# Attention weights of batches 1 to 7 transposed by DMA instead of TensorE, in a fused sliding-window attention and feed-forward kernel

## The chip, the cores and the metric

The kernel runs on one core of a Trainium2 chip. The metric is device time in microseconds; before the change it was 381.18 us (median of 3 runs, 380.14 to 381.52). The engines are called PE (TensorE, matmul), DVE (VectorE), ACT (ScalarE), POOL (GpSimd) and SP (SyncE, which here only issues DMAs).

## The reference

Two stages follow each other. The first is causal attention with a window of 64 keys, for 8 batches, 8 heads, 576 positions and 64 values per head:

```python
scores = (1 / np.sqrt(64)) * np.matmul(q, k.transpose(0, 1, 3, 2))
rel = pos[:, None] - pos[None, :]
scores = np.where((rel >= 0) & (rel < 64), scores, -1e9)
scores = scores - scores.max(axis=-1, keepdims=True)
attn = np.exp(scores); attn = attn / (attn.sum(axis=-1, keepdims=True) + 1e-09)
x = np.matmul(attn, v)              # then transposed and reshaped to (8 * 576, 8 * 64) = (4608, 512)
```

The second is a feed-forward stage on the 4608 tokens, 512 to 2048 to 512:

```python
h = x @ w_in                        # (4608, 2048)
out = (h * np.cos(h)) @ w_out       # (4608, 512), float32
```

## The kernel before

**Feed-forward.** The tokens are worked on in nine tiles of 512, called mt 0 to 8. For each tile PE first makes 16 blocks `h_ps` (4 matmuls each, over the 4 head pairs, `ks`), ACT takes the sine of each block (`sin`, the cosine by a shift of pi/2) and DVE multiplies (`gT`). Then PE makes four blocks `out_ps` of 128 tokens (`ms` 0 to 3, 16 matmuls each), which DVE and ACT copy out in turn and SP stores. The input of a tile is `xT`, one slice for each of the 4 head pairs, which the attention writes.

**Attention.** It runs one batch ahead. A batch has 12 groups: 4 head pairs `p` times 3 groups `g` of three blocks of 64 queries (for both heads of the pair, so 128 rows). A group goes through `g_scores` (PE writes the mask and the scores into a PSUM bank `s_ps`, DVE takes the row maximum `negm`), `g_exp` (ACT, three exponentials `e` with their sums), `g_norm` (DVE reciprocal `rden`, then POOL writes the normalised weights `w`, 128x384 in bf16), and `g_trans`: PE transposes the three 128x128 blocks of `w` into PSUM (`tw_ps`, L179) and DVE copies them to `wT` in SBUF (L181). `values(mt, p)` then multiplies `wT` with the values `v` for the eight query blocks of 64 that tile mt and pair p need (16 matmuls, `o_ps`, L194), and ACT casts the result into `xT` (L197). `tr_q`, `tr_k` transpose q and k of the next batch on PE (`tq_ps`, `tk_ps`, L104), `put_q`, `put_k` copy them to SBUF (DVE and ACT for q, ACT for k).

**Order.** There is no scheduler: the program order on every engine is the order in which the code is written out. `at(time, fn, ...)` puts a piece of attention work into `plan` with a time in slots; `pump(time)` writes out all that is due. A tile has T = 32 slots: one after each `h_ps` block and one after each four `out_ps` matmuls. `pump` runs once more ahead of each tile, up to the time of the last `values` which that tile needs, but at least to slot 31 of the tile before; what is due later than slot 31 otherwise falls behind the first `h_ps` blocks of the next tile. Group `i` of batch `t+1` has its scores at slot 14.6 + 1.25 i of tile `t` (1.05 i for t = 0), and the other steps at fixed lags behind. So tile 1 needs all 12 groups of batch 1, tiles 2, 3 and 4 need groups 0 to 7 of batch 2, 3 and 4, and tiles 5, 6 and 7 only groups 0 to 3 of theirs; the other groups are needed one tile later.

**Queues and buffers.** SP issues the `v<-v` copies (`spread_v`, L90 and L91, two of 256 KB for each batch, after the loads of v have landed), the stores of the result (L355), and nothing else; POOL issues all loads from HBM and casts them. PSUM has eight banks: five named ones (`O1`, `X0`, `X1`, `S`, `O0`) for `h_ps`, `s_ps` and `out_ps`, one (`V`) for `o_ps`, and two in the pool `ps_t` that `tq_ps`, `tk_ps` and `tw_ps` take in turn. `wT` has 20 buffers and `w` 8.

Of the kernel before, what the change touches and what calls it, by code (L numbers as in the profile page):

```python
# [14 lines left out]
F32 = mybir.dt.float32  # L15
BF16 = mybir.dt.bfloat16
# [3 lines left out]
PSUM = bass.MemoryType.PSUM  # L20
# [5 lines left out]
GU = 3  # L26
NG = NU // GU
PAIRS = 4
Q = 16
T = 2 * Q  # L30
# [3 lines left out]
def kernel(  # L34
# [9 lines left out]
    nc = tc.nc  # L44
# [6 lines left out]
    MT = 512  # L51
# [6 lines left out]
    att = ctx.enter_context(tc.tile_pool(name="att", bufs=3))  # L58
    moe = ctx.enter_context(tc.tile_pool(name="moe", bufs=2))
    ps = ctx.enter_context(tc.tile_pool(name="ps", bufs=1, space=PSUM))  # L60
    ps_t = ctx.enter_context(tc.tile_pool(name="ps_t", bufs=2, space=PSUM))

    st = {}

# [5 lines left out]
    def bank(which, name):  # L70
        return ps.tile([128, 512], F32, tag=which, name=name)
# [102 lines left out]

    def g_trans(b, p, g):
        w = st.pop(("w", b, p, g))
        t_ps = ps_t.tile([128, GU, 128], BF16, tag="t", name="tw_ps")
        for u in range(GU):
            nc.tensor.transpose(t_ps[:, u], w[:, u], ident)  # L179
        wT = att.tile([128, GU, 128], BF16, tag="wT", name="wT", bufs=20)  # L180
        nc.vector.tensor_copy(wT, t_ps)  # L181
        st["wT", b, p, g] = wT


    def values(mt, p):
        if ("xT", mt) not in st:
            st["xT", mt] = att.tile([128, PAIRS, MT], BF16, tag="xT", name="xT", bufs=2)
        o_ps = bank("V", "o_ps")
        for i in range(TU):
            b, j = divmod(mt * TU + i, NU)  # L190
            wT = st["wT", b, p, j // GU]
            w = wT[:, j % GU].rearrange("k (t h) -> k t h", h=2)
            for h in range(2):
                nc.tensor.matmul(out=o_ps[64 * h:64 * h + 64, 64 * i:64 * i + 64],  # L194
                                 lhsT=vtiles[b % 2][:, j, 128 * p + 64 * h:128 * p + 64 * h + 64],
                                 rhs=w[:, :, h], start=True, stop=True, skip_group_check=True)
        nc.scalar.copy(st["xT", mt][:, p], o_ps)  # L197
# [4 lines left out]
    def at(time, fn, *args):  # L202
        plan.append((time, len(plan), fn, args))
# [7 lines left out]
    trans_at = {}  # L211
    order_in_half = {}

    def group(time, b, p, g, lags, n):
        for lag, fn in zip(lags, (g_scores, g_exp, g_norm, g_trans)):
            at(time + lag, fn, b, p, g)
        trans_at[b, p, g] = time + lags[-1]
        order_in_half[b, p, g] = n
# [17 lines left out]
    order = [(b, p, g) for b in range(1, B) for g in range(NG) for p in range(PAIRS)]  # L236
    for t, count in enumerate((12, 12, 12, 12, 12, 12, 12)):
        pitch = 1.05 if t == 0 else 1.25
        for i in range(count):
            group(T * t + Q - 1.4 + pitch * i, *order.pop(0), (0, 1, 2.6, 5.5), i)  # L240

    for b in range(1, B):
        t0 = T * (b - 1)
# [13 lines left out]
    for mt in range(n_mt):  # L257
        for p in range(PAIRS):
            need = [divmod(mt * TU + i, NU) for i in range(TU)]
            at(max(trans_at[b, p, j // GU] for b, j in need) + 2, values, mt, p)  # L260


    qtiles = [const.tile([128, S, 2], BF16, name=f"qT{i}") for i in range(2 * PAIRS)]
# [12 lines left out]
    ident = const.tile([128, 128], BF16, name="ident")  # L276
# [41 lines left out]
    for mt in range(n_mt):  # L318
# [18 lines left out]
        for ms in range(MT // 128):  # L337
            e = ms % 2
            o_ps = bank(("O1", "O0")[ms % 2], "out_ps")
            if e == 0:  # L340
                o_sb = moe.tile([128, 2, d_model], F32, tag="out", name="out_sb")
            for ff in range(n_ff):
                nc.tensor.matmul(out=o_ps, lhsT=gT[ff // 2][:, ff % 2, ms * 128:ms * 128 + 128],  # L343
                                 rhs=w_out_sb[:, ff], start=ff == 0, stop=ff == n_ff - 1)
                if ff % 4 == 3:
# [5 lines left out]
                    if ff == n_ff - 1 and (e or mt == n_mt - 1):  # L351
# [4 lines left out]
                                          in_=o_sb[:, rows])  # L356
# [31 lines left out]
```

## Time and profile before

| | |
|---|---|
| time, median of 3 runs | 381.18 us (380.14 to 381.52) |
| the profiled execution | 381.3 us, its span 379.4 us |
| mean granted TensorE clock | 0.989 |
| busy: PE, ACT, DVE, POOL | 341.6, 277.6, 231.0, 183.4 us |
| h_ps and out_ps matmuls (L332, L343) | 133.6 and 137.4 us |
| tw_ps transposes (L179), x288 | 33.2 us busy, 227 ns for one |
| wT copies (L181), x96 | 33.3 us busy, 347 ns for one |
| DMA queues | q0 (issued by POOL) 18.36 MB, q1 (issued by SP) 13.63 MB |

The time of the profiled execution is 1.9 us above its span, for what lies outside of the first and last instruction. A busy time of PE counts each matmul with its modelled end, so matmuls that follow each other overlap in it: the distance from the start of one to the start of the next is what a matmul costs on PE.

### The profile page before, as it was taken

What the parts mean: (1) busy time and instruction counts of PE and PEld (TensorE: products, weight loads), DVE (VectorE), ACT (ScalarE), POOL (GpSimd) and SP (SyncE); (2) the same over time, 40 slices, a digit from 0 to 9 for tenths busy, and PEclk for the clock granted to TensorE, in tenths of its full rate; (3) what the DMA queues carried; (4) which work ended last, traced back from release to release, by engine and by line L of the source; (5) the groups of instructions that cost most, each with busy time, mean ns of one, the idle gap of its engine ahead of it and who ended that gap; (6) DMA issues with size and microseconds to landing.
All of it is one profiled execution on the core that took longest, in us unless ns stands there. A gap on an engine that the chain in (4) does not pass through costs nothing.

```text
span 379.4 us, 7751 instructions
## 1 busy us (share of the span) xinstructions
PE 341.6 (90%) x2736; PEld 187.7 (49%) x2784; DVE 231.0 (61%) x504; ACT 277.6 (73%) x852; POOL 183.4 (48%) x242
## 2 busy tenths in 40 slices
PE   1587878989999999989998999899989999999995
PEld 0464434644555455645564456445644565444442
DVE  8863566737863776468655866577557755632830
ACT  1786678967899679967997799778977898722620
POOL 8679903793166906691569244952582143000000
PEclk9998999989999999999999999999999999999999
DMA  8999990169011951097019901591139011003002
GB/s 117 185 223 206 190 135 2 56 119 182 0 59 57 141 103 56 15 168 119 2 56 154 147 1 58 110 160 29 58 73 103 2 59 55 2 0 112 1 28 85
DMA packets 63287, 32.49 MB, mean 86 GB/s; under 512 B 38672, under 2 KB 58640, under 8 KB 63248
## 3 DMA queue, kind: packets, MB, share of 16 engines
q0 software_dynamic: 53968, 18.36, 44.0%
q1 hardware_dynamic: 9280, 13.63, 11.0%
q8 instruction: 22, 0.36, 0.4%
q14 instruction: 17, 0.14, 0.1%
HBM read 36.70 MB, written 9.44 MB: 122 GB/s over the span
## 4 chain that ended last, share of the span: by engine, by line
PE 69%; ACT 15%; DVE 11%; issue 3%; POOL 1%; POOLq 0%
PE h_ps L332 27%; PE out_ps L343 26%; ACT e L162 6%; DVE qT L118 4%; PE tw_ps L179 4%; DVE gT L335 3%; PE s_ps L136 3%; PE o_ps L194 3%; PE s_ps L151 3%; ACT qT L116 2%; ACT sin L334 2%; PE tq_ps L104 2%; ACT L334 2%; PE tk_ps L104 2%; ACT xT L197 1%
## 5 line engine op out<-in xcount | busy, mean ns | idle before, releaser
L171 POOL TENSOR_TENSOR w<-e,rden 128x384 bf16<-128x384 f32 x96 | 78.8, 827 | 134.1 <-DVE rden L169 126.4
L343 PE MATMUL out_ps<-w_out,gT 128*128 128x512 bf16 x547 | 137.4, 379 | 1.8 <-issue 0.5
L332 PE MATMUL h_ps<-xT,w_in 128*128 128x512 bf16 x557 | 133.6, 383 | 1.6 <-issue 0.7
L335 DVE TENSOR_TENSOR gT<-h_ps,sin 128x512 bf16<-128x512 f32 x144 | 97.4, 688 | 59.5 <-ACT sin L334 59.5
L162 ACT ACTIVATE e<-s_ps,negm 128x128 f32<-128x128 f32 x288 | 103.1, 395 | 3.6 <-DVE rden L169 2.8
L334 ACT ACTIVATE sin<-h_ps 128x512 f32<-128x512 f32 x144 | 83.8, 601 | 23.4 <-PE h_ps L332 22.3
L332 PEld LDWEIGHTS <-w_in 128*128 128x128 bf16 x576 | 53.8, 99 | 57.0 <-issue 2.5
L343 PEld LDWEIGHTS <-gT 128*128 128x128 bf16 x576 | 51.2, 98 | 42.9
L154 DVE TENSOR_REDUCE negm<-s_ps 128x3 f32<-128x384 f32 x96 | 52.4, 553 | 24.4 <-PE s_ps L151 23.7
L162 ACT ACTIVATION_READ_ACCUMULATOR e<-s_ps,negm 128x1 f32 x288 | 67.1, 233 | 0.0
L181 DVE COPY wT<-tw_ps 128x384 bf16<-128x384 bf16 x96 | 33.3, 347 | 23.6 <-PE tw_ps L179 23.4
L179 PE MATMUL tw_ps<-ident,w 128*128 128x128 bf16 x288 | 33.2, 227 | 10.9 <-DVE wT L181 7.9
L116 ACT ACTIVATE qT<-tq_ps 64x576 bf16<-64x576 bf16 x32 | 25.9, 810 | 19.4 <-DVE qT L118 16.9
L136 PE MATMUL s_ps<-mask,ident 128*128 128x384 bf16 x96 | 33.7, 351 | 3.3 <-DVE gT L335 1.7
L179 PEld LDWEIGHTS <-w 128*128 128x128 bf16 x288 | 22.3, 101 | 26.8 <-issue 12.3
L84 POOL DMA_DIRECT2D v<-in_v_dram x40 | 34.3, 872 | 0.0
L151 PE MATMUL s_ps<-kT,qT 128*128 128x128 bf16 x256 | 32.0, 230 | 0.0
L350 ACT COPY out_sb<-out_ps 128x512 f32<-128x512 f32 x18 | 11.1, 617 | 28.5 <-PE out_ps L343 28.2
L118 DVE TENSOR_SCALAR qT<-tq_ps 64x576 bf16<-64x576 bf16 x32 | 25.3, 791 | 4.9 <-PE tq_ps L104 4.8
L151 PEld LDWEIGHTS <-qT 128*128 128x128 bf16 x256 | 21.6, 104 | 12.6 <-issue 2.8
L104 PE MATMUL tq_ps<-ident,q 96*128 96x96 bf16 x192 | 14.7, 217 | 13.4 <-DVE q L97 11.7
L130 ACT COPY kT<-tk_ps 128x576 bf16<-128x576 bf16 x30 | 19.3, 643 | 8.5 <-PE tk_ps L104 8.5
(37 smaller groups left out, 245.3 us busy)
## 6 DMA issues: line engine op xcount, KB each, us to landing
out_dram<-out_sb SPq DMA_DIRECT2D x16, 512.0 KB, 3.0
qc<-in_q_dram POOLq DMA_DIRECT2D x16, 288.0 KB, 4.7
kc<-in_k_dram POOLq DMA_DIRECT2D x16, 288.0 KB, 6.5
v<-in_v_dram POOLq DMA_DIRECT2D x32, 128.0 KB, 5.4
v<-v SPq DMA_DIRECT2D x16, 256.0 KB, 6.2
w_out<-in_moe_w_out_dram POOLq DMA_DIRECT2D x2, 1024.0 KB, 15.1
w_in<-in_moe_w_in_dram POOLq DMA_DIRECT2D x2, 768.0 KB, 12.6
out_dram<-out_sb SPq DMA_DIRECT2D x4, 256.0 KB, 2.0
```

What stands on the lines that cost most here:

```text
L84: nc.gpsimd.dma_start(out=vt.rearrange("p (h d) -> p h d", h=H), in_=v[b, :, c * 128:c * 128 + n, :].rearrange("h p d -> p h d"))
L118: nc.vector.tensor_scalar(to, st["tq", b, p][d], scale, None, ALU.mult)
L136: nc.tensor.matmul(out=s_ps.rearrange("p u c -> p (u c)"), lhsT=ident, rhs=mask[:, g:g + GU].rearrange("p u c -> p (u c)"), start=True, st ...
L151: nc.tensor.matmul(out=s_ps[:, u].rearrange("p (a t) -> p a t", a=2), lhsT=lhsT, rhs=rhs, start=False, stop=last, skip_group_check=True)
L154: nc.vector.tensor_reduce(out=negm, in_=s_ps, op=ALU.max, axis=AX.X, negate=True)
L162: nc.scalar.activation(e[:, u], s_ps[:, u], AF.Exp, bias=negm[:, u:u + 1], accum_out=den[:, u:u + 1])
L171: nc.gpsimd.tensor_tensor(out=w, in0=e, in1=rden.unsqueeze(2).to_broadcast([128, GU, 128]), op=ALU.mult)
L179: nc.tensor.transpose(t_ps[:, u], w[:, u], ident)
L332: nc.tensor.matmul(out=h_ps, lhsT=w_in_sb[:, ks, ff * 128:ff * 128 + 128], rhs=xT[:, ks], start=ks == 0, stop=ks == PAIRS - 1)
L334: nc.scalar.activation(sin, h_ps, AF.Sin, bias=math.pi / 2.0)
L335: nc.vector.tensor_tensor(out=gt[:, e], in0=h_ps, in1=sin, op=ALU.mult)
L343: nc.tensor.matmul(out=o_ps, lhsT=gT[ff // 2][:, ff % 2, ms * 128:ms * 128 + 128], rhs=w_out_sb[:, ff], start=ff == 0, stop=ff == n_ff - 1)
```

## The change

For batches 1 to 7, `g_trans` issues one transposing DMA from SBUF to SBUF on SP in place of three PE transposes and a DVE copy. It does so at lag 3 behind the scores, where it was 5.5, and `values` follow seven slots later instead of two: they stand at lag 10 instead of 7.5. Batch 0 keeps its way. `o_ps` gives up its own bank and takes its place in the pool `ps_t`, which now has three.

```diff
-    ps_t = ctx.enter_context(tc.tile_pool(name="ps_t", bufs=2, space=PSUM))
+    ps_t = ctx.enter_context(tc.tile_pool(name="ps_t", bufs=3, space=PSUM))
...
     def g_trans(b, p, g):
         w = st.pop(("w", b, p, g))
-        t_ps = ps_t.tile([128, GU, 128], BF16, tag="t", name="tw_ps")
-        for u in range(GU):
-            nc.tensor.transpose(t_ps[:, u], w[:, u], ident)
         wT = att.tile([128, GU, 128], BF16, tag="wT", name="wT", bufs=20)
-        nc.vector.tensor_copy(wT, t_ps)
+        if b == 0:
+            t_ps = ps_t.tile([128, GU, 128], BF16, tag="t", name="tw_ps")
+            for u in range(GU):
+                nc.tensor.transpose(t_ps[:, u], w[:, u], ident)
+            nc.vector.tensor_copy(wT, t_ps)
+        else:
+            nc.sync.dma_start(out=wT, in_=w.rearrange("p u c -> p (u c)"), transpose=True)
...
-        o_ps = bank("V", "o_ps")
+        o_ps = ps_t.tile([128, MT], F32, tag="t", name="o_ps")
...
-            group(T * t + Q - 1.4 + pitch * i, *order.pop(0), (0, 1, 2.6, 5.5), i)
+            group(T * t + Q - 1.4 + pitch * i, *order.pop(0), (0, 1, 2.6, 3), i)
...
-            at(max(trans_at[b, p, j // GU] for b, j in need) + 2, values, mt, p)
+            at(max(trans_at[b, p, j // GU] + (7 if b else 2) for b, j in need), values, mt, p)
```

What this does to the order is seen at two places. The first is SP's own row of DMAs, from the copies of v of batch 2 in tile 1 to those of batch 3 in tile 2 (`v_83` and `v_84` are the two buffers of v; DMAHW names the counter of a DMA that SP issued eight DMAs earlier, Pool the end of `w`). Before:

```order
L90 DMA v_83<-v_83 64x4x512
L91 DMA v_83<-v_83 64x4x512
L355 DMA out_dram<-out_sb 128x2x512 x2
L90 DMA v_84<-v_84 64x4x512
L91 DMA v_84<-v_84 64x4x512
```

Now:

```order
L90 DMA v_83<-v_83 64x4x512
L91 DMA v_83<-v_83 64x4x512
L184 DMA_TRANSPOSE wT<-w 128x3x128 x4
L358 DMA out_dram<-out_sb 128x2x512
L184 DMA_TRANSPOSE wT<-w 128x3x128 x6
L358 DMA out_dram<-out_sb 128x2x512
L184 DMA_TRANSPOSE wT<-w 128x3x128 x2
L90 DMA v_84<-v_84 64x4x512
L91 DMA v_84<-v_84 64x4x512
```

Twelve transposing DMAs a batch stand between the copies of v: four ahead of the first store, six between the stores and two behind the second. In tile 0 it is five, seven and none. Each waits in SP's row for its `w` and for the DMA that SP issued eight places earlier.

The second place is ACT at the end of tile 1, from the last exponentials of batch 2 to the sines of tile 2 (`qT_81` is the q of the third pair of the next batch). Before:

```order
L197 CAST xT<-o_ps 128x512 [waits PE_49]
L162 ACTIVATE e,den<-s_ps,negm 128x128 [waits DVE_49,Pool_49]
L162 ACTIVATE e,den<-s_ps,negm 128x128 x2
L197 CAST xT<-o_ps 128x512 [waits PE_49]
L350 COPY out_sb<-out_ps 128x512 [waits DMAHW5_49,PE_49]
L197 CAST xT<-o_ps 128x512 [waits PE_49]
L334 ACT_TABLE_LOAD
L334 ACTIVATE sin<-h_ps 128x512 [waits PE_49] x2
L116 ACTIVATE qT_81<-tq_ps 64x576 [waits DVE_49]
L334 ACTIVATE sin<-h_ps 128x512 [waits PE_49] x2
```

Now:

```order
L162 ACTIVATE e,den<-s_ps,negm 128x128 [waits DVE_49,Pool_49]
L162 ACTIVATE e,den<-s_ps,negm 128x128 x2
L200 CAST xT<-o_ps 128x512 [waits PE_49]
L353 COPY out_sb<-out_ps 128x512 [waits DMAHW1_49,PE_49]
L200 CAST xT<-o_ps 128x512 [waits PE_49] x2
L116 ACTIVATE qT_81<-tq_ps 64x576 [waits DVE_49]
L200 CAST xT<-o_ps 128x512 [waits PE_49]
L337 ACT_TABLE_LOAD
L337 ACTIVATE sin<-h_ps 128x512 [waits PE_49] x4
L337 ACTIVATE sin<-h_ps 128x512 [waits DVE_49,PE_49]
```

All four casts of the tile now stand behind the last exponential, and the copy `qT_81` has moved from behind the second sine of the next tile to a place ahead of the last cast. On PE the same holds: the third `tq_ps` of the next batch now stands between the values of pairs 1 and 2, ahead of the tile's first `h_ps`. At the ends of tiles 2 and 3 it is the same.

## The prediction

> **What bounds the kernel now.** I read the page first: busy times, the chain that ended last, the DMA queues.
>
> ```profile
> PE 341.6 (90%) x2736; PEld 187.7 (49%) x2784; DVE 231.0 (61%) x504; ACT 277.6 (73%) x852; POOL 183.4 (48%) x242
> DMA  8999990169011951097019901591139011003002
> q0 software_dynamic: 53968, 18.36, 44.0%
> q1 hardware_dynamic: 9280, 13.63, 11.0%
> PE 69%; ACT 15%; DVE 11%; issue 3%; POOL 1%; POOLq 0%
> ```
>
> PE carries the chain, and the DMA engines swing between full and idle. The second view is busy time by stretch, over one round of a middle tile (tile 3) and its two parts: from the first scores to the first sine's table load, and from there to the next scores.
>
> ```profile
> 165.30:205.00 39.70, 37.74 (x320) 20.91 (x324) 25.97 (x58) 33.14 (x105) 22.90 (x30) 1.00 0.59 86
> 177.20:200.20 23.00, 22.73 (x227) 13.43 (x230) 14.63 (x39) 20.69 (x84) 11.67 (x15) 1.00 0.09 31
> 179.20:194.00 14.80, 14.58 (x116) 8.52 (x116) 10.28 (x27) 14.64 (x65) 8.10 (x10) 1.00 0.10 37
> 194.00:200.20 6.20, 6.15 (x99) 3.75 (x99) 2.52 (x9) 5.45 (x20) 3.57 (x5) 1.00 0.01 3
> 200.20:216.80 16.60, 14.92 (x93) 7.47 (x94) 11.27 (x19) 12.41 (x21) 11.20 (x15) 1.00 1.28 161
> ```
>
> The columns are the length, then PE, PEld, DVE, ACT, POOL, the clock, the DMA share and GB/s. A tile takes 39.7 us and PE has no more than 2 us of it free. In the attention part two engines are full: PE, and for 14.8 us ACT as well (14.64 busy). DMA has a tenth of its engines in use there; its load falls into the first part. The third view is what PE waits for, from 60 us on, where the changed batches lie.
>
> ```profile
> PE tw_ps L179 <- DVE wT L181: 7.9, 10, 1.3
> ```
>
> These ten waits are two at the start of each of tiles 2 to 6: groups 9 to 11 have their transposes after the tile's first matmuls, and DVE, which must empty `tw_ps`, stands in its row at a `gT` that waits for the first sine. The fourth view is PE by time, in tile 3 and at its end.
>
> ```profile
> 159.85 1.12 PE L332 MATMUL h_ps<-xT,w_in 128*128 128x512 bf16 x4
> 163.49 0.33 PE L179 MATMUL tw_ps<-ident,w 128*128 128x128 bf16 x3 [1.23 <-DVE wT L181]
> 189.76 0.42 PE L104 MATMUL tq_ps<-ident,q 96*128 96x96 bf16 x6
> 190.02 0.33 PE L136 MATMUL s_ps<-mask,ident 128*128 128x384 bf16 x1
> 191.21 0.33 PE L179 MATMUL tw_ps<-ident,w 128*128 128x128 bf16 x3
> 191.38 0.33 PE L136 MATMUL s_ps<-mask,ident 128*128 128x384 bf16 x1
> 191.71 1.03 PE L343 MATMUL out_ps<-w_out,gT 128*128 128x512 bf16 x4
> 192.57 0.33 PE L179 MATMUL tw_ps<-ident,w 128*128 128x128 bf16 x3
> 199.14 0.44 PE L194 MATMUL o_ps<-wT,v 128*64 128x64 bf16 x16
> 199.51 0.82 PE L332 MATMUL h_ps<-xT,w_in 128*128 128x512 bf16 x3
> ```
>
> From start to start, three transposes cost 0.17 us (191.21 to 191.38), four large matmuls 0.86, six transposes of q 0.26, sixteen value matmuls 0.37.
>
> **The change, part by part.**
>
> *Transposes off PE.* 7 batches x 12 groups = 84 trios at 0.165 us: 13.9 us, all on the path, since PE is full. *The waits for `tw_ps`* go: 7.9 us. What stands behind them is `h_ps`, with five banks, so PE can run 4.3 us (5 x 0.86) before it needs the first `gT`; the wait of 1.23 does not come back there. *The DVE copies*, 84 x 0.347 us = 29 us, count nothing: DVE is 61% busy and its row was waited for only in the 7.9 already counted. *`o_ps` in a pool of three* instead of its own bank: nothing; between two of its users lie casts of 0.6 us that ACT has done by then.
>
> *Tile 1* needs all 12 groups of batch 1, so the last transposing DMA stands between POOL and the tile.
>
> ```profile
> 61.20 0.82 POOL L171 TENSOR_TENSOR w<-e,rden 128x384 bf16<-128x384 f32 x1 [13.37 <-DVE rden L169]
> 77.11 0.82 POOL L171 TENSOR_TENSOR w<-e,rden 128x384 bf16<-128x384 f32 x1
> 81.33 0.64 PE L194 MATMUL o_ps<-wT,v 128*64 128x64 bf16 x16 [0.67 <-ACT xT L197]
> 182.06 0.82 POOL L171 TENSOR_TENSOR w<-e,rden 128x384 bf16<-128x384 f32 x1 [10.34 <-DVE rden L169]
> 192.69 0.83 POOL L171 TENSOR_TENSOR w<-e,rden 128x384 bf16<-128x384 f32 x1 [0.19 <-DVE rden L169]
> 199.62 0.59 ACT L197 CAST xT<-o_ps 128x512 bf16<-128x512 f32 x1
> 200.23 1.28 ACT L334 ACT_TABLE_LOAD   x1
> 191.06 0.81 ACT L116 ACTIVATE qT<-tq_ps 64x576 bf16<-64x576 bf16 x1
> ```
>
> The rows are, in order, the first and last `w` of batch 1, the last values for tile 1, the first and eighth `w` in tile 3, the last cast there with the table load behind it, and a copy of q. The last `w` of batch 1 ends at 77.9. With 2.2 us to landing (below) the last values start at 80.1, where they started at 81.33: 1.2 us gained. The trios have 2.0 of this tile in the sum, so 0.8 goes back.
>
> *Tiles 2, 3, 4.* The values now come last, and with them a copy of q that stood behind the tile's start. PE loses nine trios before that place (1.5 us) and gains a `tq_ps` (0.26): it is at the last values at 197.9 and at `h_ps` at 198.3, done with three of the four matmuls at 198.9. ACT is not so early: between 179.2 and 200.2 it is busy 20.1 us (14.64 + 5.45 by stretch), has 0.9 free and gets 0.81 more, so its last cast still ends at about 200.1. PE waits 1.2 us for it, three times: 3.6 us back. ACT thus holds the attention part, and the gain of those tiles lies in their first part. Tiles 5 to 7 need groups 0 to 3 only and have no such wait.
>
> *The DMA itself* is what the trace of before does not show. Its nearest rows:
>
> ```profile
> out_dram<-out_sb SPq DMA_DIRECT2D x16, 512.0 KB, 3.0
> v<-v SPq DMA_DIRECT2D x16, 256.0 KB, 6.2
> out_dram<-out_sb SPq DMA_DIRECT2D x4, 256.0 KB, 2.0
> ```
>
> ```profile
> L90 SPq DMA_DIRECT2D v<-v x8: 590/597/702, 14.4 to 289.0; - x8
> DMA to landing us min/median/max: 3.2/6.2/7.4
> ```
>
> One moves 128x384x2 = 98,304 bytes. What counts is p, the time after which SP's row lets the next one go. Low end: SP is held 0.6 us by a copy of 256 KB. High end: each takes the 6.2 us to landing of `v<-v` (a copy inside SBUF, beside loads), one by one. Nearest is the cost of a packet: q0 has 0.44 x 16 x 379.4 / 53968 = 49 ns for packets of 340 bytes, q1 0.11 x 16 x 379.4 / 9280 = 72 ns for 1.5 KB. Cut in rows of 256 bytes (one block's row) the DMA has 384 pieces: 384 x 49 / 16 = 1.2 us, which I take, with 2.2 us to landing, a little over the 2.0 of the lone store. Then the queue is free each time: in tile 0, `w` comes every 1.45 us (61.2 to 77.1 in eleven steps), in tile 3 every 1.5. A store between them holds SP some 0.6 us more, which the free quarter microsecond of the next steps takes up. POOL's eight buffers of `w`, which the DMA now frees instead of PE, last for twelve microseconds at that pace. Eight DMAs may be open, so that limit is not met either.
>
> The sum: 13.9 + 7.9 - 0.8 - 3.6 = 17.4 us off the profiled execution's 381.3, which stands 0.1 above the median: 363.9, or **364**.
>
> How long p may be: in tile 0 the twelfth is done at 62.0 + 12p, landed 1.0 later, against the 80.1 of the sum: 12p - 17.1 us lost. In tiles 1 to 3 the eighth lands at 182.9 + 8p + 1.0, against 199.5, from where ACT's cast is late: 8p - 15.6 lost, three times. Together 36p - 63.9; at p = 2.3 (36 x 2.26) the gain of 17.4 is gone.
>
> [...]
>
> **The rivals.**
>
> *SP's row becomes the bound (the other side).* If the DMA is cut finer, in 768 pieces of 128 bytes, at q1's 72 ns, p = 3.5. Then tile 1 starts 24.9 us late, tiles 2 to 4 12.4 each (37.2), and the fourth group of tiles 4 to 6 lands at 182.9 + 14 + 1 = 197.9, about 3.4 after PE would be at its values: 10 more. 381.3 - 17.4 + 72 = 436 us. For it: PE's values wait in PE's row, and all of the feed-forward behind them. Against it: q0's cheaper packets and idle DMA engines in that stretch. It decides from p = 2.3 on.
>
> *Late landing without a queue.* At 6.2 us to landing, but pipelined, tile 1 loses 4.0 (6.2 - 2.2) and tiles 2 to 4 0.2 each (193.5 + 6.2 = 199.7): 368.5. For it: that is the median of `v<-v`. Against it: those copies run beside loads.
>
> *ACT holds the attention part of every tile.* Then the eight trios in it are worth nothing in tiles 4 to 6 either: 3 x 1.3 = 3.9 back, 368. For it: the 14.64 of 14.80; against it: in those tiles no cast has to come before the next `h_ps`.
>
> That SP would not do what the diff says can be left out: 84 transposing DMAs are in its row, and 504 rows are gone from PE's.
>
> **How the numbers follow.** The likeliest case, p up to 1.9, has 0.49, late landing 0.06, ACT 0.06, p of 2.0 to 2.4 0.07 (0.02 faster, 0.05 within 0.5%), SP's row as bound 0.32. Within 0.5% (1.9 us) a measurement of this kernel could not be told from no change. So faster 0.63, same 0.05, slower 0.32. The likeliest case has 360 to 369: the waits of 3.6 may not come, or p may be 1.7 (3.3 in tile 1). The range over all cases goes from 359 to 402, which is p = 2.84; beyond it lie some 0.17 above and 0.03 below.
>
> **What would show it.** Right: 36 `tw_ps` on PE instead of 288; no wait for `wT`; `v<-v`, stores and transposes in SP's row with gaps; the starts of tiles 5 and 6 about 36 us apart. Wrong: PE idle at `o_ps` for a DMA of `wT`, ahead of tiles 1 to 4 above all; SP held for over 2.3 us by each transpose, or the eighth in a batch landing more than 7 us after its `w`; then the time is near the slow rival, and the starts of tiles 2 to 5 are more than 40 us apart.

## The result, and the profile after

The changed kernel takes 365.59 us (median of 4 runs, 363.55 to 368.88), beside 381.35 us (380.14 to 381.71) for the kernel before in the same rounds: a ratio of 0.960, with a 95% interval of 0.956 to 0.963, so 15.8 us are gained. The profiled execution took 365.88 us, its span is 364.0. The runs of this kernel lie further apart (5.3 us) than those of the kernel before (1.6); what may be behind it is said further down.

First the page: the busy times, the granted clock and the DMA share over the span, the queues and the chain that ended last.

```profile
PE 329.6 (91%) x2532; PEld 172.0 (47%) x2532; DVE 206.6 (57%) x420; ACT 273.5 (75%) x852; POOL 183.0 (50%) x242
PEclk9999998976999999999999999999999999999999
DMA  8999991599015793479449935495459064002002
q0 software_dynamic: 53968, 18.36, 46.9%
q1 hardware_dynamic: 44224, 21.90, 25.8%
PE 56%; ACT 21%; DVE 13%; issue 5%; DMA 3%; POOL 2%; ACTq 0%; POOLq 0%
```

PE is as full as before. It lost 12 us of busy time by the pages, and in truth more: the trace of before lacks 48 of the 1152 `h_ps` and `out_ps` matmuls (its page has 557 and 547 of 576 each), and this one lacks none. The chain now has 3% of DMA. The clock has its deepest dip in the ninth and tenth slice (72.8 to 91 us). Queue q1 has 44224 packets where it had 9280; 34944 more over 84 DMAs are 416 each, which is 384 and 32 more.

The transposing DMAs by themselves, in SP's row: the duration columns are the shortest, median and longest time in ns for which one held SP, and below is the time from issue to landing.

```profile
L184 SPq DMA_TRANSPOSE wT<-w x84: 1177/1207/2348, 59.9 to 306.1; - x84
DMA to landing us min/median/max: 2.3/2.4/9.1
```

The median is what the sum had (1.2 and 2.2); the longest is not. What PE waits for, from 60 to 330 us, in total, times and longest:

```profile
PE o_ps L197 <- DMA wT<-w: 5.5, 3, 4.5
PE h_ps L335 <- ACT xT L200: 2.2, 3, 0.7
PE s_ps L136 <- ACT e L162: 1.3, 6, 0.3
PE o_ps L197 <- ACT xT L200: 0.8, 4, 0.2
```

The 7.9 us at `tw_ps` are gone, and 5.5 us for a DMA of `wT` have come, three waits in all. All three are ahead of tile 1. PE by time there, with the loads that POOL issues beside it:

```profile
75.13 0.22 PE L197 MATMUL o_ps<-wT,v 128*64 128x64 bf16 x2 [0.33 <-DMA wT<-w]
75.13 0.71 POOL L77 DMA_DIRECT2D qc<-in_q_dram  x1
75.84 0.67 POOL L77 DMA_DIRECT2D kc<-in_k_dram  x1
76.50 1.80 POOL L84 DMA_DIRECT2D v<-in_v_dram  x2
77.61 0.64 PE L197 MATMUL o_ps<-wT,v 128*64 128x64 bf16 x16 [0.66 <-DMA wT<-w]
79.04 2.46 POOL L84 DMA_DIRECT2D v<-in_v_dram  x3
82.78 0.26 PE L197 MATMUL o_ps<-wT,v 128*64 128x64 bf16 x2 [4.53 <-DMA wT<-w]
82.98 10.25 PE L335 MATMUL h_ps<-xT,w_in 128*128 128x512 bf16 x36
```

The DMA that ends the 4.53 us was the last of batch 1. This is that one DMA in its line's view, cut to 76 to 78 us:

```profile
L184 SPq DMA_TRANSPOSE wT<-w x1: 1901/1901/1901, 75.4 to 75.4; - x1
DMA to landing us min/median/max: 7.3/7.3/7.3
```

Issued at 75.4, it landed at 82.7, where the median DMA would have landed at 77.8. Busy time by microsecond there (columns as in the stretches of before: length, PE, PEld, DVE, ACT, POOL, clock, DMA share, GB/s) shows what runs beside it and what it leaves behind:

```profile
75.00:76.00 1.00, 0.28 (x4) 0.26 (x4) 0.05 (x1) 0.89 (x2) 1.00 (x3) 1.00 0.52 109
77.00:78.00 1.00, 0.39 (x15) 0.39 (x16) 0.00 (x0) 0.61 (x2) 1.00 (x2) 0.72 0.78 91
78.00:79.00 1.00, 0.25 (x9) 0.12 (x6) 0.00 (x0) 0.50 (x1) 1.00 (x2) 0.50 1.27 184
80.00:81.00 1.00, 0.00 (x0) 0.00 (x0) 0.00 (x0) 0.00 (x0) 1.00 (x2) 0.50 1.18 166
86.00:87.00 1.00, 1.00 (x4) 0.39 (x3) 0.30 (x1) 0.39 (x1) 0.00 (x0) 0.50 2.14 169
87.00:88.00 1.00, 1.00 (x4) 0.37 (x3) 0.69 (x1) 0.20 (x1) 0.00 (x0) 0.66 1.31 203
```

The DMA engines, which had a share of 0.01 in the stretch that the forecast read (the end of tile 3), fill up here from 75 us on (the share is the time that the packets took over that of 16 engines; it reaches 2.82 from 81 to 82 us), and the clock granted to PE is at half from about 77.4 to 87.7 us (from the shares of 0.72 and 0.66): PE starts tile 1 at 82.98 and works its first 4.7 us at half speed. The kernel before has a shorter stretch of half clock at the same place, from about 81.2 to 84.7 us; one microsecond of it:

```profile
82.00:83.00 1.00, 0.69 (x2) 0.33 (x4) 0.00 (x0) 0.96 (x3) 1.00 (x2) 0.50 0.96 137
```

Tile 3 is what a middle tile looks like now; the second row is the start of tile 2 after its first three matmuls, where the forecast had a wait of 1.2 us for ACT's cast:

```profile
157.89:194.77 36.88, 35.75 (x294) 18.85 (x289) 22.69 (x46) 32.78 (x105) 22.76 (x30) 1.00 0.87 127
122.57 1.67 PE L335 MATMUL h_ps<-xT,w_in 128*128 128x512 bf16 x7 [0.73 <-ACT xT L200]
```

The distances between the first `h_ps` of successive tiles, read from PE by time (the record at tile 5 of before is missing, so that two tiles stand together), in us:

| | start of tile 0 | tile 0 | 1 | 2 | 3 | 4 and 5 | 6 | 7 to the end |
|---|---|---|---|---|---|---|---|---|
| before | 34.95 | 47.36 | 37.87 | 39.67 | 39.66 | 79.63 | 38.56 | 61.7 |
| after | 32.51 | 50.47 | 38.03 | 36.88 | 36.88 | 73.00 | 35.34 | 60.9 |

Of the 15.4 us between the spans, 2.4 come ahead of tile 0, 15.4 in tiles 2 to 6 and 0.8 at the end; tile 0 gives 3.1 back and tile 1 0.2.

### The profile page after: what moved, and what is told of

It reads as the page before. It is cut to its first block, busy times and chain, and to the rows that moved or that the text cites. A ratio compares the mean times of both kernels' runs of the same rounds, so it can differ in the third digit from the quotient of the medians.

```text
span 364.0 us, 7402 instructions
## 1 busy us (share of the span) xinstructions
PE 329.6 (91%) x2532; PEld 172.0 (47%) x2532; DVE 206.6 (57%) x420; ACT 273.5 (75%) x852; POOL 183.0 (50%) x242
## 3 DMA queue, kind: packets, MB, share of 16 engines
q1 hardware_dynamic: 44224, 21.90, 25.8%
## 4 chain that ended last, share of the span: by engine, by line
PE 56%; ACT 21%; DVE 13%; issue 5%; DMA 3%; POOL 2%; ACTq 0%; POOLq 0%
PE h_ps L335 23%; PE out_ps L346 22%; ACT e L162 8%; DVE gT L338 5%; ACT qT L116 4%; DVE qT L118 3%; ACT sin L337 3%; PE s_ps L136 3%; PE s_ps L151 3%; DMA wT<-w 3%; ACT xT L200 2%; PE o_ps L197 2%; PE tq_ps L104 2%; POOL w L171 1%; DVE qT L276 1%
## 5 line engine op out<-in xcount | busy, mean ns | idle before, releaser
L346 PE MATMUL out_ps<-w_out,gT 128*128 128x512 bf16 x576 | 141.4, 382 | 0.0
L338 DVE TENSOR_TENSOR gT<-h_ps,sin 128x512 bf16<-128x512 f32 x144 | 95.0, 686 | 65.2 <-ACT sin L337 64.9
L337 ACT ACTIVATE sin<-h_ps 128x512 f32<-128x512 f32 x144 | 82.0, 606 | 20.1 <-PE h_ps L335 19.3
L335 PEld LDWEIGHTS <-w_in 128*128 128x128 bf16 x576 | 54.6, 99 | 67.8 <-issue 10.0
L162 ACT ACTIVATION_READ_ACCUMULATOR e<-s_ps,negm 128x1 f32 x288 | 70.5, 245 | 0.0
L200 ACT CAST xT<-o_ps 128x512 bf16<-128x512 f32 x36 | 21.8, 621 | 7.6 <-PE o_ps L197 7.4
L169 DVE RECIPROCAL rden<-den 128x3 f32<-128x3 f32 x96 | 16.1, 168 | 17.1 <-ACT e L162 15.7
L104 PE MATMUL tq_ps<-ident,q 96*128 96x96 bf16 x192 | 14.4, 215 | 11.7 <-DVE q L97 11.7
L97 POOL COPY k<-kc 96x768 bf16<-96x768 bf16 x28 | 23.4, 836 | 1.8 <-DMA kc<-in_k_dram 1.8
```

Of the source, the lines that this page charges most:

```text
L162: nc.scalar.activation(e[:, u], s_ps[:, u], AF.Exp, bias=negm[:, u:u + 1], accum_out=den[:, u:u + 1])
L335: nc.tensor.matmul(out=h_ps, lhsT=w_in_sb[:, ks, ff * 128:ff * 128 + 128], rhs=xT[:, ks], start=ks == 0, stop=ks == PAIRS - 1)
L337: nc.scalar.activation(sin, h_ps, AF.Sin, bias=math.pi / 2.0)
L338: nc.vector.tensor_tensor(out=gt[:, e], in0=h_ps, in1=sin, op=ALU.mult)
```

## The experiments

Each edit is against the changed kernel, except the first, which is against the kernel before, and those for which the text names another. Times are medians; ratios are to the kernel before, with 95% intervals.

### The PSUM part alone

```diff
-    ps_t = ctx.enter_context(tc.tile_pool(name="ps_t", bufs=2, space=PSUM))
+    ps_t = ctx.enter_context(tc.tile_pool(name="ps_t", bufs=3, space=PSUM))
-        o_ps = bank("V", "o_ps")
+        o_ps = ps_t.tile([128, MT], F32, tag="t", name="o_ps")
```

> The kernel before with one part of the change alone: the values' output o_ps in the pool of three PSUM banks instead of its own bank; transposes stay on TensorE at their old place. Theory A: this part brought the earlier start of tile 0 that the changed kernel shows (first h_ps at 32.5 us instead of 35.0), since the values of tile 0 follow each other without matmuls between them: first h_ps at 32.5, time 379.0 us against 381.4. Rival (the prediction's step): it is worth nothing, first h_ps at 35.0, time 381.4 us.

Measured: 373.12 us, ratio 0.977 (0.975 to 0.979). This is 8.2 us of the 15.8, with every transpose still on PE, and more than either theory gave. The waits of PE from 60 to 330 us in this kernel:

```profile
PE tk_ps L104 <- DVE wT L181: 1.7, 5, 0.3
PE h_ps L332 <- ACT xT L197: 1.1, 1, 1.1
PE tw_ps L179 <- DVE wT L181: 1.0, 5, 0.2
```

The 7.9 at `tw_ps` are 1.0, because a third buffer lets PE write on while DVE stands at its `gT`. The tiles say where the 8.2 lie: tile 0 starts 2.0 us earlier (32.96), is 1.0 shorter, tiles 2 and 3 are 38.62 and 38.63 (1.05 and 1.03 shorter), tiles 4 to 6 give 3.5, and tile 1 gives 0.3 back.

### No transposition at all after batch 0

Leaves out the transposition of the weights of batches 1 to 7: the values use `w` as it is. Order and PSUM stay as changed; `w` of these batches gets 20 buffers of its own, as `wT` had, since the values now hold it longer.

```diff
         else:
-            nc.sync.dma_start(out=wT, in_=w.rearrange("p u c -> p (u c)"), transpose=True)
+            wT = w
```

> The changed kernel with the transposition of batches 1 to 7 left out altogether: the values multiply with the untransposed weights, no DMA, no matmul, no copy. Theory A: the transposing DMAs cost time only ahead of tile 1, where TensorE waits 4.5 us for one and its clock then falls to half for some 9 us: first h_ps of tile 1 at about 78.5 us instead of 83.0, no half clock behind it, 357 us in all against 365.6, and the distances of tiles 2 to 6 as in the changed kernel (36.9, 36.9, 36.5, 36.5). Rival: the DMAs slow the middle tiles too (through the loads beside them): their distances fall below 36.3 and the time below 354. Other rival: the wait ahead of tile 1 hides another one: above 361.

Measured: 359.42 us, ratio 0.942 (0.941 to 0.944): all the DMAs together cost 6.2 us. Tiles 2 to 5 take 36.88, 36.89, 36.48 and 36.53, to 0.01 us what they take with the DMAs (36.88, 36.88, 36.48, 36.52), so there the DMAs cost nothing. Tile 1 starts at 78.35 where it started at 82.98, and takes 36.21 where it took 38.03: 4.6 and 1.8 us, together 6.4, which is all of it. Its first matmuls show the full clock:

```profile
78.35 8.43 PE L335 MATMUL h_ps<-xT,w_in 128*128 128x512 bf16 x36
```

The same 36 matmuls took 10.25 us after the wait.

### The last four groups that tile 1 needs back on PE

```diff
+    def on_pe(b, g):
+        return b == 0 or (b, g) == (1, 2)
-        if b == 0:
+        if on_pe(b, g):
...
-            group(..., (0, 1, 2.6, 3), i)
+            group(..., (0, 1, 2.6, 5.5 if on_pe(b, g) else 3), i)
...
-            at(max(trans_at[b, p, j // GU] + (7 if b else 2) for b, j in need), values, mt, p)
+            at(max(trans_at[b, p, j // GU] + (2 if on_pe(b, j // GU) else 7) for b, j in need), values, mt, p)
```

> The changed kernel, but the last four groups of batch 1 (g = 2) keep their transposes on TensorE at the old lags; only these are needed at once, for tile 1. Theory A: TensorE's wait ahead of tile 1 goes from 5.5 us to under 1, the clock stays up, the first h_ps of tile 1 comes at 79 us: 358 us against 365.6. Rival: the clock falls there anyway and tile 1 starts at 82 as in the kernel before, which had no such wait: 364 to 366.

Measured: 359.83 us (358.89 to 359.89), ratio 0.943 (0.941 to 0.944). Four of 84 groups on PE take back 5.8 us; no transposition at all is only 0.4 us faster. Ahead of tile 1 there is no wait for a DMA left:

```profile
77.61 0.86 PE L339 MATMUL h_ps<-xT,w_in 128*128 128x512 bf16 x3
79.54 2.97 PE L339 MATMUL h_ps<-xT,w_in 128*128 128x512 bf16 x13 [1.06 <-ACT xT L203]
```

The clock is 1.00 in every microsecond from 75 to 89 us, over the start of tile 1, and the runs lie within 1.0 us instead of 5.3. It is the best of the versions that leave nothing out, 5.8 us below the changed kernel.

### What makes that DMA late: two runs

The first leaves out the loads of v for batch 2, so that the values of that batch are those of older data; the second leaves out these and the copies `v<-v` of that batch as well, and sets the first half of q and k of batch 3 to zero instead of loading it.

```diff
+            if b != 2:
                 at(t0 + (4 if b == 1 else 2) + c, load_v, b, c)
```

> The changed kernel without the loads of v for batch 2 (five DMAs, left out; the values of that batch use the v of batch 0). They are issued between 76.5 and 80.8 us, just when the last transposing DMA of batch 1 is under way. Theory A: it is these loads that make the DMA land 7 us after its issue instead of 2.4: without them TensorE waits at most 2 us, the first h_ps of tile 1 comes at 80 us, the clock stays up: 360 us against 365.6. Rival: the loads of q and k of batch 3 (issued at 75.1 and 75.8) or SyncE's own row do it: the wait stays above 3.5 us, 365 us.

Measured: 366.64 us, ratio 0.961 (0.958 to 0.963). The theory fell: a wait of 4.9 us remained.

```profile
85.07 0.27 PE L197 MATMUL o_ps<-wT,v 128*64 128x64 bf16 x2 [4.92 <-DMA wT<-w]
```

The last DMA, issued at 76.9, landed after 8.1 us. The loads of q and k stood beside it as before (issued at 76.93 and 77.64), and the copies `v<-v`, which no longer wait for loads of v, moved up beside it (79.75 and 80.46, in the changed kernel 87.00 and 87.71).

```diff
+        if (b, hb) == (3, 0):
+            nc.gpsimd.memset(t, 0.0)
+        else:
             nc.gpsimd.dma_start(out=t..., in_=src[b, hb * 4:hb * 4 + 4]...)
...
+        if b != 2:
             at(t0 + 13, spread_v, b)
```

> The changed kernel with nothing else on the DMA engines while the last transposing DMAs of batch 1 run: v of batch 2 is neither loaded nor copied, and the first half of q and k of batch 3 is set to zero by GpSimd instead of being loaded. Theory A: loads beside it are what makes the last DMA land 7 us after its issue; leaving out v alone only let the loads of q, k and the copies of v come earlier. Now it lands in under 3.5 us, the first h_ps of tile 1 comes at 80 us, no half clock: 359 to 361 us. Rival: the DMA is slow for a cause of its own (SyncE's row, the store ahead of it): wait above 3.5 us and 365 us, as with v alone left out.

Measured: 360.95 us, ratio 0.945 (0.944 to 0.947). With less traffic beside them (a DMA share of 0.03 to 0.56 from 75 to 79 us), the last two DMAs of batch 1 landed 3.8 and 2.9 us after their issue, and tile 1 started at 79.52:

```profile
78.69 0.67 PE L200 MATMUL o_ps<-wT,v 128*64 128x64 bf16 x18 [0.75 <-DMA wT<-w]
80.00:81.00 1.00, 1.00 (x4) 0.30 (x2) 0.00 (x0) 0.98 (x2) 1.00 (x2) 0.50 0.51 191
83.00:84.00 1.00, 1.00 (x6) 0.39 (x4) 0.69 (x1) 0.42 (x2) 0.21 (x1) 0.97 1.04 151
```

So it is the traffic beside it that delays the DMA, and not SP's row, which is as it was: SP was held 1.8 us by this DMA, as it was 1.9 by the late one. The loads of q and k are the only transfers that stood beside both late DMAs and not beside this one, next to which a store ran as in the other two; whether they would do it alone no run tells. The clock went to half here too, for 3.4 us.

### Every transposing DMA twice

The second one goes into a tile that nothing reads.

```diff
             nc.sync.dma_start(out=wT, in_=w..., transpose=True)
+            w2 = att.tile([128, GU, 128], BF16, tag="w2", name="w2", bufs=8)
+            nc.sync.dma_start(out=w2, in_=w..., transpose=True)
```

> The changed kernel with each transposing DMA issued twice, the second time into tiles that nobody reads, so that SyncE is held 2.4 us for each group instead of 1.2. The prediction's formula for the slow rival: with p = 2.4 a loss of 36p - 63.9 = 22 us, most of it ahead of tile 1 (11.7) and tiles 2 to 4 (3.6 each): 388 us. Rival: the DMAs that nobody waits for fill gaps of SyncE's row, and the values' seven slots cover the rest: under 375.

Measured: 432.66 us, ratio 1.134 (1.129 to 1.138), with a mean clock of 0.904. The formula of the prediction gave 388. At tile 1 it seems to hold, with a start that moved from 82.98 to 94.17, 11.2 us for the formula's 11.7; but the formula counts from a start that no late landing delays, and from the 78.35 without transposition it is 15.8. Behind it, it does not hold at all: tiles 1 to 3 took 50.74, 48.62 and 49.06 us, some 12 more each where the formula has 3.6. The waits of PE from 60 to 330 us, the last values ahead of tile 2, and the stretch around them:

```profile
PE o_ps L199 <- DMA wT<-w: 46.2, 12, 14.6
142.50 0.64 PE L199 MATMUL o_ps<-wT,v 128*64 128x64 bf16 x16 [6.64 <-DMA wT<-w]
134.00:138.00 4.00, 1.86 (x33) 1.35 (x33) 0.79 (x1) 1.16 (x2) 3.52 (x5) 0.50 1.09 129
138.00:142.00 4.00, 0.00 (x0) 0.00 (x0) 0.00 (x0) 0.00 (x0) 0.00 (x0) 0.50 1.88 173
142.00:146.00 4.00, 2.04 (x25) 1.17 (x25) 0.00 (x0) 2.37 (x4) 2.78 (x4) 0.50 1.43 140
```

Once PE stalls, the DMA engines are full between 138 and 142 us while no engine computes, DMAs of 125 to 142 us land after 7.8 us at the longest, and the clock is at half. The queue of the rival was priced; the landing beside other traffic and the clock that follow it were not.

### Values sooner

```diff
-  + (7 if b else 2)
+  + (4.5 if b else 2)
```

> The changed kernel with the values 4.5 slots behind the transposing DMA instead of 7, that is at their place of the kernel before. Theory A: a DMA lands 2.4 us after its issue, so 4.5 slots (some 5 us) are enough in tiles 1 to 6, and the 0.9 us that TensorE waits at the starts of tiles 2, 3 and 4 for ScalarE's cast behind the copy of q go away: 3 x 0.9 = 2.7 us less, 363 us. Rival: the seven slots are needed; TensorE then waits for wT ahead of the values of tiles 2 to 6, about 1 us a group, 368 us or more.

Measured: 369.48 us, ratio 0.969 (0.965 to 0.972): slower than the changed kernel, where the theory had it faster. The profiled execution (367.37) is the fastest of the six, so its trace shows 1.5 of the 3.9 us. In it the loss is not in tiles 2 to 6: tile 1 starts at 84.00, 1.0 later, and tile 7 is 1.8 longer, with a wait of 1.57 us for a DMA. Two waits ahead of tile 1:

```profile
79.07 0.45 PE L197 MATMUL o_ps<-wT,v 128*64 128x64 bf16 x16 [2.12 <-DMA wT<-w]
83.81 0.27 PE L197 MATMUL o_ps<-wT,v 128*64 128x64 bf16 x2 [4.29 <-DMA wT<-w]
```

The same was tried, with five slots for the seven, on the kernel that has the four groups on PE (its `7` becomes `5`).

> As e4_b1g2_pe (batch 1's last four groups on TensorE), and the values 5 slots behind a transposing DMA instead of 7. Theory A: with the collision ahead of tile 1 gone, the five slots cover the 2.4 us to landing everywhere, and about 0.5 us comes off each of the starts of tiles 2, 3 and 4, where the values moved out from behind the copy of q: 358.3 us against 359.8. Rival: waits for wT come up, 361 or more.

Measured: 362.23 us, ratio 0.949 (0.947 to 0.951), 2.4 slower than with seven. Tiles 2 and 3 get 0.48 and 0.32 shorter, as the theory had. But PE waits twice for a DMA, 1.03 us in tile 1 and 1.25 in tile 7, and tiles 4 to 6 grow by some 0.35 each. Of the distances tried, seven slots are the best.

### The PSUM part undone

```diff
-    ps_t = ctx.enter_context(tc.tile_pool(name="ps_t", bufs=3, space=PSUM))
+    ps_t = ctx.enter_context(tc.tile_pool(name="ps_t", bufs=2, space=PSUM))
-        o_ps = ps_t.tile([128, MT], F32, tag="t", name="o_ps")
+        o_ps = bank("V", "o_ps")
```

> The changed kernel with its PSUM part undone: o_ps has its own bank again, ps_t two. Theory A: the PSUM part alone gave 8.3 us on the kernel before because a third bank ends the waits of tw_ps for DVE's copy; with the transposes gone from TensorE these waits are gone in any case, so undoing it costs only the 2 to 2.5 us at the start of tile 0: 368 us against 365.6. Rival: the two parts add up, and undoing it costs the 8.3: 373.5.

Measured: 370.00 us, ratio 0.970 (0.968 to 0.973), 4.4 slower than the changed kernel, between the two theories. Tile 0 starts at 34.71 (2.2 later), tile 1 takes 39.68 (1.65 more), and tiles 2 and 3 take 37.66 (0.78 more). Its waits from 60 to 330 us:

```profile
PE o_ps L197 <- ACT xT L200: 6.8, 12, 2.0
PE o_ps L197 <- DMA wT<-w: 1.5, 1, 1.5
```

The late values of a tile come in a pile, and with one bank each waits for ACT's cast of the one ahead. So the parts do not add up: the third bank is worth 8.2 us with the transposes on PE, and 4.4 without them.

### The late order with the transposes on PE

As the changed kernel, but all transposes on PE with DVE's copy, at lag 5.5, the values at the same lag of 10.

> The changed kernel with its transposes back on TensorE (lag 5.5, with DVE's copy), but the values at their new, late place and o_ps in the pool of three. Beside e1_psum (373.1 us, the same with the values at the old place) it shows what the lateness costs by itself. Theory A: the copy of q ahead of the last cast and the pile of values at the tile's end cost about 0.9 us at the starts of tiles 1 to 4: 376.5 us. Rival: the lateness costs nothing here, 373.

Measured: 373.85 us (372.49 to 374.48), ratio 0.979 (0.977 to 0.981), beside 373.12 for the PSUM part alone. By the medians the late place costs 0.7 us; the two profiled spans stand the other way round (370.5 and 371.2). It costs or gains no more than that.

### The copy of q behind the tile's start again

On the kernel with the four groups on PE, the transposition of the third pair of the next q and k two slots later, which takes the copy of q out from ahead of the last cast.

```diff
-            time = t0 + (3.4 * p if b == 1 else 7.5 * p - 15)
+            time = t0 + (3.4 * p if b == 1 else 7.5 * p - 15 + (2 if p == 2 else 0))
```

> As e4_b1g2_pe, with one more edit: the third pair's q and k of the next batch two slots later, behind the start of the tile, so that ScalarE casts the last values without the copy of q ahead of it. Theory A: the 0.74 to 1.06 us that TensorE waits at the starts of tiles 1 to 4 for that cast goes (3.3 us): 356.5 us against 359.8. Rival: ScalarE is as late by its exponentials alone, or the copy of q now holds up the sines: within 1 us of 359.8.

Measured: 359.86 us, ratio 0.943 (0.941 to 0.944), beside 359.83: no gain. The wait for the cast is gone, as meant. The start of tile 4 in the kernel without this edit (first two rows), and with it (third):

```profile
188.63 0.82 PE L339 MATMUL h_ps<-xT,w_in 128*128 128x512 bf16 x3
190.18 2.97 PE L339 MATMUL h_ps<-xT,w_in 128*128 128x512 bf16 x13 [0.73 <-ACT xT L203]
187.90 3.55 PE L339 MATMUL h_ps<-xT,w_in 128*128 128x512 bf16 x11
```

Tile 4 starts 0.73 us earlier, and tile 5 starts at 225.11 in both. In between, PE waits for ACT's exponentials until the same moment. That wait, and what ACT waits for DVE's half of the copy of q from 187 to 226 us, without the edit and then with it:

```profile
211.74 0.32 PE L136 MATMUL s_ps<-mask,ident 128*128 128x384 bf16 x1 [0.21 <-ACT e L162]
211.74 0.32 PE L136 MATMUL s_ps<-mask,ident 128*128 128x384 bf16 x1 [0.27 <-ACT e L162]
ACT qT L116 <- DVE qT L118: 0.3, 1, 0.3
ACT qT L116 <- DVE qT L118: 2.5, 2, 1.5
```

So the copy of q, now among the sines, holds ACT up there; this is the rival's second half. Still, the edit is worth something in this trace. From the start of tile 0 to that of tile 5 it takes 0.8 us off (191.74 for 192.53); this execution started tile 0 0.79 us later, ahead of anything that the edit moves. The mean clock of its runs was lower as well (0.985 to 0.986 in all four, 0.993 to 0.995 without the edit); what they would take at an equal clock is not known.

## Why the prediction was right, and where it was wrong

The forecast of 364.0 us was 1.6 us too low and on the right side. Its steps, one by one:

| step of the prediction | its size | measured | by |
|---|---|---|---|
| p, SP held by one DMA | 1.2 us, in 384 pieces | 1.207, 416 packets, 32 more than the pieces | profile after |
| landing | 2.2 | 2.4 median, 7.3 where it counted | profile after |
| trios off PE, less the waits for the cast | 13.9 - 3.6 = 10.3 | 14.4 (12.7 by the profiled spans) | 373.85 to 359.42 |
| waits for `tw_ps`; pool of three "nothing" | 7.9 | 8.2, by the pool alone | 381.4 to 373.12 |
| late order | in the waits above | -0.7 | 373.12 to 373.85 |
| tile 1 | -0.8 | -6.2 | 359.42 to 365.59 |

The measured column sums to 8.2 - 0.7 + 14.4 - 6.2 = 15.7 us, the predicted one to 17.4. The total came out near because errors of 4.1 and 5.4 us stand against each other, which is luck. The split also hangs on the order of the steps: with the pool taken last, it is worth 4.4 us and all the rest 11.4 (the run at 370.00).

**Right, and in part by luck.** The DMA's own price was the step with the widest bounds. SP is held 1.2 us, and the 416 packets of a DMA are 32 more than the 384 pieces. But the 49 ns for each, taken from q0, are not: by the pages, q1 went from 11.0% of 16 engines in 379.4 us to 25.8% in 364.0, which is 835 us for 34944 packets, 24 ns for one. The packets of one DMA thus take 0.6 us of the 16 engines, and SP is held for 1.2, twice that; by what, no run shows. That the two figures met is luck. Right without luck is the rest of it: from tile 2 on the DMAs cost nothing, and tiles 4 and 5 are 36.5 us long, about as said.

**Tile 1: the term that was mis-sized.** The sum let the last DMA land after 2.2 us, and it took 7.3. It also had SP's row free each time, and the row held this DMA 1.0 us: its `w` ended at 74.4 and SP, which takes up seven of these DMAs some 1.3 us apart there, came to it at 75.4. So one of the prediction's signs of being wrong did appear, PE idle at `o_ps` for a DMA ahead of tile 1; ahead of tiles 2 to 4 there is none. The share of busy DMA engines had been read at the end of tile 3 (0.01). At the end of tile 0 the trace of before showed otherwise: POOL issues the loads of q, k and v right behind the last `w` of the batch, and the microsecond in which the forecast has the DMA land (80.1) was not idle.

```profile
77.11 0.82 POOL L171 TENSOR_TENSOR w<-e,rden 128x384 bf16<-128x384 f32 x1
78.64 0.71 POOL L77 DMA_DIRECT2D qc<-in_q_dram  x1
80.00:81.00 1.00, 0.52 (x18) 0.44 (x17) 0.92 (x2) 0.47 (x2) 1.00 (x3) 1.00 1.02 309
```

The first of these rows stood in the prediction; the two behind it did not. This is the mechanism of the rival "late landing without a queue", which had 4.0 us at tile 1 and a chance of 0.06. What it left out as well is the clock: 1.8 of the 6.2 us are matmuls at half speed behind the wait. The trace of before had half clock at this place too (0.50 from 82 to 83 us), and the sum did not price it. A landing on the path would also explain why the runs spread by 5.3 us, where the kernel without that wait spreads by 1.0; their single landings were not traced, and the slowest run has the lowest mean clock (0.977, the fastest 0.989), so this is argued and not shown.

**PSUM: the wrong cause for the right size.** The waits for `tw_ps` were counted to the transposes, and the pool of three to "nothing". The pool alone ends nearly all of them. Of its 8.2 us, 5.6 lie in tiles 2 to 6, where the waits were; 3.0 are the earlier start of tile 0 and tile 0 itself, which no step had. So the nearness of 7.9 and 8.2 is luck too. The view of waits named the bank (`tw_ps`, waiting for the copy that frees it); that a third bank would end them as well as no transposes stood in that row and was not asked.

**The waits for the cast.** They came, at 0.73 and 0.19 us for each of three tiles instead of 1.2. Most of that belongs to the late order and not to the trios: in that order PE waits 2.2 us for casts with the transposes on PE, and 3.0 with none. Taking them off PE adds 0.8 us of such waits where the sum had 3.6. What the waits cost by themselves is not shown. The run that ends them made ACT wait elsewhere, and in tile 4 PE met ACT's exponentials no earlier. So the reason behind the subtraction, that a wait of PE on its full path must cost what it lasts, does not hold there: the next meeting with ACT takes the time back.

**The slow rival.** It was real, its break-even was not. With each DMA doubled (2.45 us of SP for a group) the formula gave 388 and the chip 432.66, where the trace has other transfers beside the late DMAs (a DMA share of 1.09 to 1.88 from 134 to 146 us) and PE at half clock behind its waits (0.50 there). If the loss grows evenly between the two p of 1.2 and 2.45, which no run shows, it crosses the gain near 1.5, well ahead of the 2.3 of the formula. So 0.32 was not too much for this case.

**The landing.** 98 KB land 2.4 us after their issue (median of 84), and the lone stores of the kernel before, from which the forecast took its 2.2, land after 2.0 us with 256 KB; how much of either is a fixed time no run shows.

## What to carry to other kernels

Before work is given to a DMA, look for the one place where its landing is awaited soonest, and read the DMA share in that very stretch; where loads run there, leave those few transfers on the engine and move the rest (here four groups of 84, which took 5.8 us off). When PE waits for a PSUM bank, price a further bank by itself before counting the wait to whatever else the change removes (here the bank alone was worth 8.2 us). And price a stall of PE with what the other queues will do in it, and with the clock after it (here 1.8 us at half clock behind a wait of 4.5).

## What was not expected of the hardware

A transposing DMA of 128x384 in bf16 whose median landing is 2.4 us took 7.3 us beside loads and a store, with the DMA share between 0.5 and 1.3 while it was under way at first (75 to 81 us) and above 2 at the end (2.82 from 81 to 82). Such landings occur later as well (7.9 us between 96 and 122 us, 9.1 between 170 and 195), but PE waits for none of them; POOL waits seven times between 85 and 330 us for a buffer of `w` that a DMA reads, 5.8 us in all and 1.1 at the longest.

The granted clock fell to half before the long wait, not because of it: at about 77.4 us, in the last of three microseconds in which PE was 28%, 76% and 39% busy, mostly with matmuls of 64 columns. It came back at about 87.7, 4.7 us after PE was full again; with nothing loaded it came back 3.5 us after. The stretch at half clock lasted 10.2 us; at the same place it lasts 3.4 us in the run with nothing loaded and in the kernel before.

In the 3.4 us ahead of the fall PE was busy 53% here, 48% with nothing loaded and 63% in the kernel before, so in all three the clock fell behind a stretch in which PE was partly busy. The busy share alone does not decide it: in the run without transposition PE was busy 47% from 52.2 to 55.7 us, and its four `out_ps` matmuls from 55.51 on took 0.87 us to the start of the next, as at full clock (0.86). What decides it no run shows.
